# The first loads of a fused attention and feed-forward kernel: how many may be under way at once

## The chip, the cores and the metric

The kernel runs on one core of one Trainium2 chip. The metric is the device time of one execution in microseconds (us). The core has a matrix engine (PE, with its weight loads shown apart as PEld), three engines for elementwise work (DVE, ACT, POOL), a control engine SyncE (SP) that issues transfers here, and 16 DMA engines that carry them out. A load is "issued" when SP has handed it over, and "lands" when its semaphore says that all its data is in on-chip memory.

## The reference

The computation is sliding-window attention followed by a two-layer feed-forward network:

```python
# q, k, v: (8, 8, 576, 64); window 32
scores = scale * np.matmul(q, k.transpose(0, 1, 3, 2))
mask = np.abs(pos[:, None] - pos[None, :]) <= window
scores = np.where(mask, scores, -1000000000.0)
attn = softmax(scores)                    # max, exp, sum written out in full
x = np.matmul(attn, v)                    # -> (4608, 512): tokens x (head, dim)
h = x @ w_in                              # (512, 2048)
r = np.maximum(h, 0.0)
out = (s * (r * r) + b) @ w_out           # (2048, 512)
```

All inputs and the output are f32; the kernel casts what it multiplies to bf16.

## The kernel before, in words

The 4608 tokens are the eight sequences, one after the other. Attention is done per sequence in units of 128 keys; the feed-forward part runs over thirteen blocks of tokens (96, 128, 128, 160, 256, 256 and then seven of 512). The first four blocks are the first sequence, so the feed-forward part of sequence 0 can begin as soon as its attention is there, and the attention of later sequences is laid between the matrix products of earlier blocks.

The order of the work is made by a small planner. Every piece of work is a `_Task` with a stream (pe, act, dve, pool, sp), a cost in ns, a key, and the tasks it depends on (`_Graph.add`, L89). `plan` (L120) simulates the streams and puts each one's tasks in an order; `emit` (L228) turns the dependences into semaphore waits. Each stream runs its tasks strictly in the order planned, so a waiting task holds up all behind it on its engine. A transfer has in `dma` a kind, the number of packets per DMA engine and the ns per packet; their product is the planner's price of it. A transfer's wait is a wait of the engine that issues it, in most cases SP.

Tasks with a key under -100 are special: they are chained (L93, L97 to L99, L116), so they keep the order in which the program adds them. These are the first loads, all issued by SP in `attention` (L931):

- eight pairs of heads of sequence 0, q and k in turn (`load_pair`, L619, issued at L623; 288 KB, price 8 packets x 113 ns). Each goes into one of eight staging buffers `stg`, is cast to bf16 (L632, L633), turned on PE (L639) and copied out (L645, L646); `pair_scores` (L853) follows.
- two units of v (`load_v`, L561, issued at L571; 256 KB, 64 packets x 20 ns), cast at L580.
- the rest of v of sequence 0 in two halves of the partitions (`load_rows`, L584, issued at L589; 320 KB each, together 32 packets x 56 ns). DVE and POOL cast them (L592), then PE puts them in place (`place_v`, L609).
- eight loads of `w_in` (`load_weights`, L532, issued at L543; 512 KB, 16 packets x 86 ns), cast by POOL at L546.
- two tiny loads of s and b (L961).
- eight loads of `w_out` (L543, 16 packets x 85 ns), cast by POOL at L546. PE uses them first in `early` (L1066, L1074) and then in the sum over all rows at L1083.
- eight pairs of sequence 1 (L623, 8 packets x 93 ns) and five units of its v (L571, 64 packets x 17 ns, the last one 32).

The eight staging buffers serve all of the pairs and weights in turn. A load therefore waits until the cast that last read its buffer is done. Besides that, what limits how far ahead SP issues is the number of semaphores of its kind (12 for these loads) and what the DMA queue takes. What comes behind the first loads on SP are the loads of later sequences (L670, L571), transposing transfers (L685, L835) and the stores of the output (L1063).

PE's matrix products of the feed-forward part are at L1025 (`w_in`) and at L1043 (`w_out`); ACT applies the relu (L1032), DVE squares (L1034).

Of the kernel before, what the change touches and what calls it, by code (L numbers as in the profile page):

```python
# [56 lines left out]
AHEAD = {"pe": 48, "act": 180, "dve": 240, "pool": 240}  # L57


class _Task:  # L60
# [3 lines left out]
    def __init__(self, n, stream, fns, cost, lat, key, dma, slack, after):  # L64
        self.slack, self.after, self.next = slack, after, []
        self.n, self.stream, self.fns, self.cost, self.lat, self.key, self.dma = \
            n, stream, fns, cost, lat, key, dma
        self.deps, self.users = set(), []
        self.ready = self.start = self.fin = 0.0
        self.sem = self.seq = self.val = None  # L70
        self.used = False
        self.snap = self.half = self.mark = None


class _Graph:
# [3 lines left out]
    STREAMS = ("pe", "act", "dve", "pool", "sp")  # L79
    LAT = {"pe": 260.0, "act": 130.0, "dve": 110.0, "pool": 150.0, "sp": 60.0}  # L80
    MARGIN = 250.0
    RING, PUSH, CALM, ISSUE, WRITE = 112.0, 95.0, 40.0, 1400.0, 600.0

    def __init__(self, queues):
        self.queues = queues
        self.tasks, self.chain = [], None
        self.writer, self.readers = {}, {}

    def add(self, stream, fns, cost, reads=(), writes=(), key=0.0, accum=False, dma=None, waits=(),  # L89
            lat=None, slack=0.0):  # L90
        if not isinstance(fns, list):
            fns = [fns]
        after = [self.chain] if key < -100 and self.chain else []  # L93
        t = _Task(len(self.tasks), stream, fns, cost, self.LAT[stream] if lat is None else lat, key,
                  dma, slack, after)
        t.deps.update(waits)
        for a in after:  # L97
            assert a.stream == stream
            a.next.append(t)  # L99
        for r in reads:  # L100
            assert r in self.writer, r
            t.deps.add(self.writer[r])
        for w in writes:
            if w in self.writer:
                t.deps.add(self.writer[w])
            if not accum:
                t.deps.update(self.readers.get(w, ()))
        t.deps.discard(t)
        for r in reads:
            self.readers.setdefault(r, []).append(t)  # L110
        for w in writes:
            self.writer[w] = t
            if not accum:
                self.readers[w] = []
        self.tasks.append(t)
        if key < -100:  # L116
            self.chain = t
        return t

    def plan(self):  # L120
# [48 lines left out]
        def release(t):  # L169
            for u in t.users:  # L170
# [7 lines left out]
                else:  # L178
                    r = t.fin + t.lat + (self.MARGIN if u.stream == "pe" else 0.0)
                u.ready = max(u.ready, r)  # L180
# [139 lines left out]
def bass_sliding_window_symmetric__then__act_starrelu_kernel(  # L320
# [23 lines left out]
    with ExitStack() as es:  # L344
# [120 lines left out]
        def zero(stream, tile, res, cost, key=-90.0):  # L465
            add(stream, lambda e: e.memset(tile, 0.0), cost, writes=[res], key=key)

        add("dve", lambda e: e.memset(ONESW[:], 1.0), 150, writes=["ONESW"], key=-99)
        add("dve", lambda e: e.memset(RECS[:], 1.0), 250, writes=[("REC", i) for i in range(NU)], key=-58)

        add("dve", lambda e: e.memset(SROW[:], 0.0), 100, writes=[("SROW", 0), ("SROW", 1)], key=-58)
# [901 lines left out]
```

## Time and profile before

| | |
|---|---|
| median of 3 runs | 319.38 us (317.86 to 321.13) |
| the profiled execution's own time | 317.84 us |
| its span, first to last instruction | 316.1 us |
| PE busy | 300.3 us (95%) |
| DVE, ACT, POOL busy | 193.7, 141.8, 90.1 us |
| moved by DMA | 56.13 MB, mean 178 GB/s |
| `w_in` loads, issue to landing, median | 9.8 us |
| `w_out` loads, issue to landing, median | 9.6 us |
| q and k pairs, issue to landing, median | 5.3 and 4.9 us |

The profile is of one execution. Its page divides the span into 40 equal slices and gives each engine's busy share in tenths; PEclk is the granted clock of PE in tenths of full speed; DMA is the mean busy share of the 16 DMA engines. The chain of waits goes back from the last instruction, at each step to what released it; cut to a stretch, each line is start, length and what it was. "SPq" is SP's sequencer issuing a transfer, and its length contains the time for which it could not hand the transfer over. "DMA vst<-in_v_dram" is the time from an issue to a landing. In the table of engines by stretch the columns are busy time of PE, PEld, DVE, ACT and POOL, each with its number of instructions, then granted clock, DMA share and GB/s.

### The profile page before, as it was taken

The numbers are of one execution on the slowest core, as the hardware profiler recorded it, in microseconds if no ns is written. First come the engines' busy times: TensorE is split into PE (matmuls) and PEld (weight loads), VectorE is DVE, ScalarE is ACT, GpSimd is POOL, SyncE is SP. The second block draws the span as 40 slices with busy tenths as digits, with TensorE's granted clock in tenths as the row PEclk, the third lists the DMA queues.
The fourth block names the chain that finished last, engine by engine and source line by source line (L and its number), as shares of the span: only waits on it lengthen the run. The fifth ranks groups of instructions, "written<-read, shape, count | busy, mean of one in ns | idle before, by whom it ended". The sixth has DMA issues, their size and how long they took to land.

```text
span 316.1 us, 8467 instructions
## 1 busy us (share of the span) xinstructions
PE 300.3 (95%) x3588; PEld 164.6 (52%) x3632; DVE 193.7 (61%) x381; ACT 141.8 (45%) x221; POOL 90.1 (29%) x108
## 2 busy tenths in 40 slices
PE   8779999989999999999999999999999999999995
PEld 3558775466764454554444444444444444444444
DVE  4447587578884886988569485875545543333312
ACT  3836435355744674764166354444444333333300
POOL 3368955528225123241412421423000000000000
PEclk9959999999999999999999999999999999999999
DMA  7999999997996998799899999989221110001022
GB/s 229 254 382 388 386 288 276 154 191 227 261 194 169 291 178 155 232 240 158 210 292 119 183 222 301 123 151 222 73 62 53 50 46 35 33 34 36 34 94 76
DMA packets 96921, 56.13 MB, mean 178 GB/s; under 512 B 71472, under 2 KB 86064, under 8 KB 96880
## 3 DMA queue, kind: packets, MB, share of 16 engines
q1 hardware_dynamic: 96880, 55.56, 75.8%
q8 instruction: 29, 0.48, 0.7%
q14 instruction: 12, 0.10, 0.1%
HBM read 36.70 MB, written 9.44 MB: 146 GB/s over the span
## 4 chain that ended last, share of the span: by engine, by line
PE 87%; DVE 3%; SPq 3%; issue 2%; DMA 2%; ACT 2%; POOL 0%; ACTq 0%; POOLq 0%
PE w L1025 37%; PE o L1043 35%; PE avn L787 4%; PE avn L1074 2%; DMA vst<-in_v_dram 2%; PE sc L729 2%; DVE gt L1034 2%; PE o L1074 2%; ACT r L1032 1%; SPq L623 1%; SPq L589 1%; PE avn L818 1%; PE w L639 1%; PE w L609 1%; SPq L571 1%
## 5 line engine op out<-in xcount | busy, mean ns | idle before, releaser
L1025 PE MATMUL w<-xt,win 128*128 128x512 bf16 (+4 forms) x814 | 139.9, 312 | 3.1 <-issue 1.4
L1032 ACT ACTIVATE r<-w 128x512 bf16<-128x512 f32 (+2 forms) x148 | 86.3, 585 | 104.2 <-PE w L1025 83.1
L1043 PE MATMUL o<-wout,gt 128*128 128x512 bf16 (+1 forms) x510 | 123.0, 372 | 1.9 <-issue 1.4
L1034 DVE TENSOR_TENSOR gt<-r 128x512 bf16<-128x512 bf16 (+2 forms) x148 | 77.7, 530 | 74.3 <-ACT r L1032 74.2
L1025 PEld LDWEIGHTS w<-xt,win 128*128 128x128 bf16 x832 | 68.9, 98 | 52.8 <-issue 0.3
L1043 PEld LDWEIGHTS o<-wout,gt 128*128 128x128 bf16 x528 | 50.7, 98 | 55.0
L695 POOL COPY kt<-ktr 128x512 bf16<-128x512 bf16 (+1 forms) x30 | 32.3, 1078 | 41.7 <-DMA ktr<-nat 40.2
L678 POOL CAST nat<-stg 128x1024 bf16<-128x1024 f32 (+1 forms) x21 | 24.5, 1165 | 59.7 <-DMA stg<-in_q_dram 39.1
L757 ACT ACTIVATE ex<-sc 128x1024 bf16<-128x1024 f32 (+1 forms) x29 | 29.6, 1022 | 24.1 <-PE avn L787 22.1
L1059 DVE SCALAR_TENSOR_TENSOR outs<-o,sb,cvec 128x512 f32<-128x512 f32 (+1 forms) x35 | 25.4, 729 | 13.1 <-PE o L1043 13.0
L761 DVE TENSOR_TENSOR ex<-ex,mask 128x1024 bf16<-128x1024 bf16 (+1 forms) x29 | 21.6, 746 | 1.3 <-ACT ex L757 0.2
L811 DVE TENSOR_TENSOR xn<-avn,rec 128x512 bf16<-128x512 f32 (+1 forms) x31 | 21.4, 690 | 1.0
L787 PE MATMUL avn<-vb,ex 64*64 64x65 bf16 x952 | 20.9, 199 | 0.3
L787 PEld LDWEIGHTS avn<-vb,ex 64*64 64x64 bf16 x952 | 13.6, 108 | 13.3 <-issue 7.6
L580 DVE CAST vb<-vst 128x512 bf16<-128x512 f32 (+1 forms) x29 | 13.2, 459 | 2.9 <-DMA vst<-in_v_dram 2.9
L678 DVE CAST nat<-stg 128x1024 bf16<-128x1024 f32 (+1 forms) x15 | 13.6, 903 | 2.2 <-DMA stg<-in_k_dram 1.3
L729 PE MATMUL sc<-qt,kt 64*64 64x128 bf16 x440 | 11.7, 216 | 0.0
L809 DVE RECIPROCAL rec<-avn 128x8 f32<-128x8 f32 (+1 forms) x31 | 6.2, 201 | 7.0 <-PE avn L787 6.8
L826 ACT COPY xt<-avn 128x512 bf16<-128x512 bf16 (+2 forms) x14 | 7.2, 523 | 6.2 <-PE avn L818 6.2
L646 DVE COPY kt<-w 128x576 bf16<-128x576 bf16 x8 | 6.0, 755 | 5.1 <-PE w L639 5.1
L639 PEld LDWEIGHTS w<-ident,nat 64*64 64x64 bf16 x288 | 6.9, 121 | 4.3 <-issue 1.7
L546 POOL CAST win<-stg 128x1024 bf16<-128x1024 f32 x8 | 8.3, 1040 | 2.7 <-DMA stg<-in_moe_w_in_dram 2.6
(100 smaller groups left out, 153.5 us busy)
## 6 DMA issues: line engine op xcount, KB each, us to landing
out_dram<-outs SPq DMA_DIRECT2D x35, 256.0 KB, 2.5
vst<-in_v_dram SPq DMA_DIRECT2D x30, 256.0 KB, 5.3
stg<-in_q_dram SPq DMA_DIRECT2D x6, 1024.0 KB, 6.0
stg<-in_k_dram SPq DMA_DIRECT2D x6, 1024.0 KB, 10.3
stg<-in_moe_w_in_dram SPq DMA_DIRECT2D x8, 512.0 KB, 9.8
stg<-in_moe_w_out_dram SPq DMA_DIRECT2D x8, 512.0 KB, 9.6
stg<-in_q_dram SPq DMA_DIRECT2D x8, 288.0 KB, 5.3
stg<-in_k_dram SPq DMA_DIRECT2D x8, 288.0 KB, 4.9
```

Of the source, the lines that this page charges most:

```text
L678: add(eng, lambda e, x=x: e.tensor_copy(nat[0:top, 1024 * x:1024 * x + 1024].rearrange("p (i h d) -> p h i d", h=H, i=2), stg[0:top, :].re ...
L695: add("pool", lambda e, c=c, w=w: e.tensor_copy(KT[slot][:, :, c:c + w].rearrange("p a (s i) -> p a s i", i=4), KTR[slot][:, :, :, c // 4: ...
L729: fns = [lambda e, pr=pr, x=x, b=b, j=j, hp=hp: e.matmul(SC[64 * x:64 * x + 64, hp, pr * 128:pr * 128 + 128], lhsT=KT[b % 2][64 * hp:64 * ...
L757: add("act", lambda e, dst=flat_dst, src=flat_src: e.activation(dst, src, AF.Exp, bias=0.0, scale=0.125), 190 + 0.833 * 512 * len(hs), rea ...
L761: add("dve", lambda e, flat=flat, mask=mask: e.tensor_tensor(flat, flat, mask, ALU.mult), 130 + 0.53 * 512 * len(hs), reads=[("E", ei, hp, ...
L787: return [lambda e: e.matmul(av[64 * x:64 * x + 64, h, 0:D + 1], lhsT=buf[64 * g:64 * g + 64, h % 2, h // 2, c:c + 64], rhs=VB[64 * g:64 * ...
L811: add("dve", lambda e: e.tensor_tensor(XN[xi][0:p1, :].rearrange("p (a c) -> p a c", a=H), av[0:p1, :, 0:D], REC[ri][0:p1, :].rearrange("p ...
L1025: add("pe", [lambda e, g=g, kc=kc: e.matmul(wt[:, g, :], lhsT=WIN_BF[:, kc, (f0 + g) * 128:(f0 + g + 1) * 128], rhs=XT[:, kc, t0 % XR:t0 % ...
L1032: add("act", lambda e: e.activation(rt, wt, AF.Relu, bias=0.0, scale=1.0), 190 + 0.833 * ng * nt, reads=[("W", wb)], writes=[("R1", rb)], ...
L1034: add("dve", lambda e: e.tensor_tensor(GT[gs][:, f0:f0 + ng, g0:g0 + nt], rt, rt, ALU.mult), 130 + 0.53 * ng * nt, reads=[("R1", rb)], wri ...
L1043: add("pe", [lambda e, fc=fc: e.matmul(O[:, ob, 0:cn], lhsT=GT[gs][:, fc, g0:g0 + 128], rhs=WOUT_BF[:, fc, c0:c0 + cn], start=(fc == 0), s ...
L1059: add("dve", lambda e: e.scalar_tensor_tensor(OUTS[us][:, 0:cn], bank, SB128[:, 0:1], CVEC[:, c0:c0 + cn], ALU.mult, ALU.add), 200 + 1.07 ...
```

## The change

Each transfer of the chain of first loads gets one more dependence, on an earlier load of that chain. `add` goes back through the earlier loads of the chain and adds up their prices (packets x ns per packet). At the first one with which the sum passes `AHEAD` = 4500 ns it stops, and the new load waits for that one to land. Three weight loads are worth 4128 ns. Loads of 64 packets or more get no such wait, but they count in the sum of those behind them. Since SP issues the loads, it is SP that waits, before it issues.

```diff
+    AHEAD = 4500.0
...
-        self.tasks, self.chain = [], None
+        self.tasks, self.chain, self.line = [], None, []
...
         t.deps.update(waits)
+        if key < -100 and dma is not None:
+            full = 0.0
+            for other in reversed(self.line):
+                full += other.dma[1] * other.dma[2]
+                if full > self.AHEAD and dma[1] < 64:
+                    t.deps.add(other)
+                    break
+            self.line.append(t)
```

The planner sees the new dependences too, so the orders of the streams could move with them.

## The prediction, made before the changed kernel ran

> **What bounds the kernel now.** I read the page's 40 slices first, then the chain of waits cut to the first 75 us, SyncE's timeline, the DMA view of three stretches, each first load's issue and landing, and what POOL waited for.
>
> ```profile
> PE   8779999989999999999999999999999999999995
> PEclk9959999999999999999999999999999999999999
> DMA  7999999997996998799899999989221110001022
> ```
>
> The span is 316.1 us, a slice 7.9 us. After the third slice PE never leaves 8 or 9, so only the start is open to anything that loads do: the first slices are weaker on PE, and the third runs at half the granted clock. DMA is full there too.
>
> ```profile
> 7.07 3.05 SPq L589
> 10.12 0.04 issue
> 10.16 6.46 DMA vst<-in_v_dram
> 16.63 0.02 issue
> 16.65 0.02 POOLq L296
> 16.67 0.08 issue
> 16.75 0.98 POOL gt L592
> 17.73 0.05 issue
> 17.78 1.25 PE w L609 x10
> ```
>
> This is the chain (start, length, what). The one transfer on it is the second half of `load_rows`: issued at 10.16, landed at 16.63, cast by POOL, then PE. The 3.05 us of SPq before it look like a cost of issuing. They are not: SyncE sits in that instruction while the DMA engines are full, as the next rows show. The first fence is the DMA view of 0 to 20 us in half-microsecond slices, the second that of 17 to 39 us.
>
> ```profile
> DMA  0001899997799999999999999999999999999999
> GB/s 0 0 0 32 230 355 392 304 286 180 207 286 300 355 378 401 410 383 344 289 258 250 182 239 223 197 230 246 207 166 196 221 369 389 385 389 406 369 381 381
> ```
>
> ```profile
> DMA  9999999999999999999999999999999999999999
> GB/s 391 384 398 369 384 391 387 387 391 380 395 384 387 387 410 361 380 387 391 387 391 380 387 387 387 391 399 376 387 380 402 380 395 372 410 364 384 392 390 405
> ```
>
> From 2 us on the engines are full but for a dip at 4.5 to 5.5 us; the weight stream runs at 387 GB/s without a hole. The first bytes move between 1.5 and 2.0 us, and the first load's issue ended at 1.20: at most 0.8 us from issue to data.
>
> ```profile
> POOL win L546 <- DMA stg<-in_moe_w_in_dram: 2.6, 5, 1.4
> POOL gt L592 <- DMA vst<-in_v_dram: 1.9, 1, 1.9
> ```
>
> ```profile
> 12.00:16.00 4.00, 2.73 (x112) 1.72 (x110) 1.31 (x3) 3.30 (x5) 0.87 (x3) 1.00 1.08 211
> 16.00:20.00 4.00, 2.22 (x20) 1.33 (x20) 2.10 (x5) 0.67 (x2) 3.02 (x3) 0.58 1.05 384
> 20.00:24.00 4.00, 3.85 (x93) 3.13 (x92) 1.61 (x4) 1.59 (x3) 2.11 (x3) 0.56 1.05 388
> 24.00:28.00 4.00, 3.79 (x88) 3.36 (x85) 3.03 (x7) 2.64 (x5) 3.37 (x4) 1.00 1.05 387
> ```
>
> Between 17 and 45 us POOL waits for loads only for `w_in`, 2.6 us in five pieces, and 1.9 us for the rows. The second table (busy PE, PEld, DVE, ACT, POOL; then granted clock, DMA share, GB/s) places PE's weak stretch: 2.73 and 2.22 of 4 us while the rows are awaited, and the clock at about a half from 16.7 to 23.5 us.
>
> **The change, part by part.** The orders of the two builds agree line by line on PE, DVE, ACT and POOL, waits included. On SyncE the order is the same too and 25 loads gain a wait for an earlier load's landing. By the code's own prices (start pairs 8x113 = 904, v 64x20 = 1280, rows 32x56 = 1792, `w_in` 16x86 = 1376, `w_out` 1360, later pairs 8x93 = 744) a load waits for the nearest one before it with which the sum passes 4500. For weights that is the fourth back; so at its release three are still to come. Loads of 64 packets (v0, v1 and four of the next five) get no wait.
>
> *Start pairs.* The sixth, seventh and eighth wait for the first, second and third. Those landed (issue plus landing time) at 0.80+2.8 = 3.6, 1.26+3.1 = 4.4 and 1.73+4.7 = 6.4 us; the issues were at 3.14, 3.62 and 4.09. The last moves by 2.3 us to about 6.5, and behind it in SyncE's queue v0 moves from 4.88 to 6.95, v1 from 5.58 to about 7.65. Who waits for v0, v1: the casts, then the first L787. Cover: the fourth to seventh pairs landed at 7.2, 8.0, 8.7, 9.5, so the eighth, whose data can start by 6.9+0.8 = 7.7, is in time, and v0's by 7.6+0.8 = 8.4 are too: the queue then still holds the seventh and eighth pair (to 9.5 and some 10.3). Cost 0. If the cover were gone, v0's whole shift of 2.07 us would reach the rows' landing and, through POOL and PE, the end one to one. The bound below zero: the third pair landed 2.0 us after the second, the later ones 0.7 to 0.8 after each other; if that excess of 1.3 us came from the depth of the queue it would go. The DMA share in 4 to 8 us is 0.97, which leaves little of either; I take 0.
>
> *Rows and the first weights.* The rows wait for the sixth pair (3.14+5.6 = 8.7); their issue ran from 7.07 to 10.12, held by the full queue, so it still ends near 10.1. The first two `w_in` loads wait for the eighth pair and v0 (some 10.3 and 11.5, estimates between the neighbours' landings); they were issued at 10.82 and 12.33: not binding. The third waits for the rows, 16.6 instead of 12.84: 3.8 us later. Its data can start at 16.65+0.47+0.8 = 17.9; the second lands at 12.33+6.6 = 18.9, so it is there 1.0 us early. Cost 0.
>
> *The other weights.* Landings run from 21.4 (third `w_in`) to 29.59+9.3 = 38.9 (last `w_out`), 13 steps, 1.35 us each. At a release three loads, 4.05 us, are ahead; wait, issue and first bytes take 0.05+0.47+0.8 = 1.3. Spare 2.7 us. So the issues move by 4 to 7 us and the landings do not. SyncE's two scalar loads now stand between the wait at 24.2 and the first `w_out`: 0.90+0.53 us (their rows), so that one is issued at 25.7 instead of 18.85, its data due at 28.1: 1.6 us to spare. If the cover went: POOL, which casts the weights, has a reserve of 0.4 us (the last `w_in` lands at 28.1, its cast starts at 28.53) and PE behind it 0.5 (the first `w_out` cast ends at 31.10, PE's first weight load of L1074 is at 31.58); beyond 0.9 us a delay goes to the end.
>
> A rule speaks against this part. The Trainium skill, "DMA: Bandwidth & Descriptors", section "Rules for kernel authors", says to issue a DMA early and wait for its semaphore late, so that the fixed setup cost overlaps; "Anatomy of one DMA" puts that cost at about 2.0 us. The first load here took 2.8 us from issue to landing with some 0.75 of it moving, which agrees. Were the 2.0 bare at each of 12 held weight loads, an estimate by that page gives 24 us and 343 us in all; three loads ahead are what the rule's overlap asks for, and by the rows it stays hidden.
>
> *Later pairs and v.* Four of the eight pairs move (31.1 to 34.9, 32.7 to 36.2, 35.8 to 37.5, 38.5 to 38.9); due from 38.9 on in turn. The others and the last v were already issued after the landing they now wait for, because POOL freed their buffer late. Cost 0. SyncE is free at 45.6 as before, so L670 behind it does not move.
>
> **Sum.** 0+0+0+0 on the profiled execution's own 317.84 us (span 316.1 and 1.7 around it). That run lies 1.5 under the median of the three shown, 319.38; I forecast 319.4.
>
> **The rivals.**
>
> *Slower: v0's shift shows.* Place: between the eighth pair and v0. It decides once v0's first bytes come after 8.5 to 9.0, where the GB/s row begins to fall from 410 (the pairs give way to the small rows of v); my estimate is 8.4, so it is close, though the slowest engines, which set a landing, are about 1.3 us further back. Price up to 2.07: 321.5; and if PE's longer pause holds the half clock for half a stretch more (3.4 us at half speed, 1.7), 323.2.
>
> *Slower: the shallow queue loses the lead of the faster engines.* The third `w_in` landed 2.5 us after the second, the others 1.35: an excess of 1.1 us, beside an instruction fetch. The DMA view shows three such packets in 10 to 30 us and three in 25 to 45, say four more that today do not show in a landing. If all did: 4.4, less the reserve of 0.9, 3.5: 322.9. Against: three loads are ahead, over 1.1 us.
>
> *Faster: the early excess goes.* 1.3 us: 318.1; if PE's shorter pause also kept the clock whole, up to half of the 5.6 us that PE worked in the slow stretch (2.22+3.85 less 0.5 after 23.5), 2.8: 315.3. Against: fewer than eight loads were queued when the excess arose.
>
> *The waits do not bind*, because buffers freed by POOL and the full queue already hold the loads: 319.4 too. True of seven waits, not of the weights.
>
> **How the numbers follow.** Forecast 0.64, waits not binding 0.08, v0's shift 0.13, lost lead 0.08, early excess gone 0.07. A measurement of this kernel tells about 1% from no change: 316.2 and 322.6. Below lie about half of the last case and a little scatter of the first: 0.07; above, half of v0's shift, most of the lost lead and some scatter: 0.18; between, 0.75. Range 316.6 (318.1 less the 1.5 by which single runs lie under the median) to 323.2; the forecast's own, 317.9 to 321.1, is the scatter of the three runs.
>
> **What would show it.** Right: `w_in` and `w_out` land in steps of 1.35 us, issue to landing down from 9.6 to about 5.5 us, DMA still 9 in all slices of 17 to 39, the rows landing near 16.6, PE's L609 near 17.8. Wrong: holes in the DMA row at 8 to 9 or behind 17 us, POOL waiting more than 2.6 us for `w_in`, or the clock row changed in slices two to four.

## The result, and the profile after

| | before | changed |
|---|---|---|
| median of 21 runs each | 318.45 us (316.80 to 321.85) | 320.94 us (318.25 to 324.49) |
| ratio, 95% interval | | 1.0071 [1.0042, 1.0099] |
| the profiled execution's own time | 317.84 us | 320.93 us |
| its span | 316.1 us | 319.2 us |
| PE's granted clock over the span | 0.989 | 0.989 |
| rows landed | 16.63 us | 16.21 us |
| last `w_in`, first and last `w_out` landed | 28.14, 29.48, 38.89 us | 29.30, 30.61, 40.38 us |
| last pair of sequence 1 landed | 44.83 us | 48.00 us |

The change costs 0.7%, about 2.3 us: less than the 1% that a measurement of this kernel was said to tell, but here the interval excludes no change. Here and below a ratio is estimated from the runs within 1.5% of their kernel's fastest, so it can differ from the quotient of the medians, which are of all runs. The forecast was 319.4 and the range 316.6 to 323.2. All lines of the code behind the edit moved by 9, so L543 of before is L552 here, L546 is L555, L1074 is L1083, L1090 is L1099; in most of the experiments they moved by one more.

The page's 40 slices of the changed kernel, 8.0 us each:

```profile
PE   7688989989979999999999999999999999999996
PEclk9969999999999999999999999999999999999999
DMA  7999998996998997999999999987111210000022
GB/s 237 267 329 359 355 319 241 190 174 163 325 171 157 301 190 146 235 253 187 187 298 153 126 239 322 153 167 169 49 52 52 67 60 35 33 34 36 34 82 86
```

PE reads 8 in the fourth and sixth slice (24 to 32, 40 to 48 us) where it read 9; the 8 in the ninth stands in both rows (7.17 us busy in 64 to 72, 7.19 before), and the 7 in the twelfth is taken up below. Only one slice is below 9 in clock, as before: the clock has no part in the loss.

The DMA view of the changed kernel, 17 to 39 us in 40 slices:

```profile
DMA  9689999899999999999999989899789999999999
GB/s 350 227 201 276 331 391 350 313 294 302 350 406 413 410 421 380 380 272 395 398 391 361 324 305 425 291 250 261 246 298 335 376 350 354 361 372 398 402 355 398
DMA packets 3901, 7.54 MB, mean 343 GB/s; under 512 B 246, under 2 KB 246, under 8 KB 3897
```

This stretch was 9 throughout and 387 GB/s. Now there are holes at 17.5 us and between 30 and 33 us, and also slices in which the engines read 9 while they move 250 to 300 GB/s: they are busy, but with slower packets. Packet by packet, most 2 KB pieces of the weights take 0.084 to 0.095 us in both kernels. In 16.5 to 38 us none of 3844 took more than 0.3 us before; in the changed kernel 57 of 3566 did (called long below), the longest 1.45 us, in bursts. Many of the bursts follow a hole (17 to 19.5 us, 31.5 to 34); those at 26.3 and 29.3 us stand where the row reads 9.

Who pays is in what PE and DVE waited for between 26 and 52 us (total, times, longest). PE in the kernel before, PE in the changed kernel, DVE in the changed kernel:

```profile
PE sc L1090 <- DVE outs L1087: 0.3, 1, 0.3
PE avn L1074 <- DVE gt L1034: 0.3, 1, 0.3
```

```profile
PE sc L1099 <- DVE outs L1096: 1.3, 1, 1.3
PE o L1083 <- POOL wout L555: 1.2, 1, 1.2
PE w L1034 <- ACT r L1041: 0.5, 2, 0.3
```

```profile
DVE nat L642 <- DMA stg<-in_k_dram: 1.6, 2, 0.8
```

PE's first product with `w_out` waits 1.2 us for POOL's cast of the first `w_out` load. That cast ended at 32.27 us (31.10 before), because the load landed at 30.61. Some 15 us later PE waits 1.3 us, 1.0 more than before, for DVE's copies of the output. DVE does its work in the planned order, and had itself stood still 1.6 us for the pairs of sequence 1, which land up to 3.2 us later. The pairs are not the only reason for that second wait, as `win_only` shows below. The two waits add 2.2 us.

The chain of waits of the changed kernel (start, length, what), cut to 8 to 50 us:

```profile
...
9.98 6.24 DMA vst<-in_v_dram
16.21 0.02 issue
16.23 4.76 DMA stg<-in_moe_w_in_dram
20.99 0.02 issue
21.00 6.97 DMA stg<-in_moe_w_in_dram
27.98 0.02 issue
27.99 5.52 DMA stg<-in_moe_w_out_dram
33.51 0.02 issue
33.52 5.20 DMA stg<-in_moe_w_out_dram
38.73 0.02 issue
38.74 6.06 DMA stg<-in_k_dram
44.80 0.02 issue
44.82 0.64 DVE nat L642
...
```

Before, this chain held one transfer and then went over to POOL and PE. Now each load is released by the landing of another: a loop through SyncE that is gone round five times after the rows, most turns four loads long.

The profiled spans differ by 3.1 us, and not all of it is in those two waits. Matched in order, ACT's instructions at 60 to 80 us start 1.1 us later than before, and 3.3 us later from 95 us on. The second step is at DVE's casts of the next q and k (L678, here L687):

```profile
DVE nat L687 <- DMA stg<-in_k_dram: 2.1, 1, 2.1
DVE nat L687 <- DMA stg<-in_q_dram: 1.5, 1, 1.5
```

The profile of before has no such wait between 78 and 95 us. One must not put it down to the change too soon, as the experiments show.

### The profile page after: what moved, and what is told of

Read it like the earlier page. It is cut to its first block, busy times and chain, and to the rows that moved or that the text cites. A ratio compares the mean times of both kernels' runs of the same rounds, so it can differ in the third digit from the quotient of the medians.

```text
span 319.2 us, 8485 instructions
## 1 busy us (share of the span) xinstructions
PE 298.8 (94%) x3588; PEld 163.0 (51%) x3632; DVE 190.3 (60%) x381; ACT 141.6 (44%) x221; POOL 90.7 (28%) x108
## 4 chain that ended last, share of the span: by engine, by line
PE 76%; DMA 17%; DVE 2%; issue 2%; SPq 1%; ACT 1%
PE o L1052 33%; PE w L1034 32%; DMA stg<-in_k_dram 7%; DMA stg<-in_moe_w_in_dram 4%; PE avn L796 3%; DMA stg<-in_moe_w_out_dram 3%; DMA vst<-in_v_dram 2%; PE sc L738 2%; PE avn L1083 2%; PE o L1083 1%; DMA stg<-in_q_dram 1%; DVE gt L1043 1%; PE w L648 1%; PE avn L827 1%; SPq L598 0%
## 5 line engine op out<-in xcount | busy, mean ns | idle before, releaser
L687 POOL CAST nat<-stg 128x1024 bf16<-128x1024 f32 (+1 forms) x21 | 25.4, 1211 | 63.7 <-DMA stg<-in_q_dram 41.8
L704 POOL COPY kt<-ktr 128x512 bf16<-128x512 bf16 (+1 forms) x30 | 31.5, 1050 | 40.3 <-DMA ktr<-nat 38.9
L766 ACT ACTIVATE ex<-sc 128x1024 bf16<-128x1024 f32 (+1 forms) x29 | 29.7, 1023 | 23.9 <-PE avn L796 21.9
L687 DVE CAST nat<-stg 128x1024 bf16<-128x1024 f32 (+1 forms) x15 | 11.0, 736 | 4.5 <-DMA stg<-in_k_dram 3.0
L555 POOL CAST win<-stg 128x1024 bf16<-128x1024 f32 x8 | 8.3, 1042 | 4.2 <-DMA stg<-in_moe_w_in_dram 4.1
L1083 PE MATMUL o<-wout,gt 128*128 128x512 bf16 x25 | 7.4, 379 | 1.8 <-POOL wout L555 1.2
L1083 PE MATMUL avn<-wout,gt 128*128 128x512 bf16 x31 | 8.7, 380 | 0.2 <-issue 0.2
```

Of the source, the lines that this page charges most:

```text
L687: add(eng, lambda e, x=x: e.tensor_copy(nat[0:top, 1024 * x:1024 * x + 1024].rearrange("p (i h d) -> p h i d", h=H, i=2), stg[0:top, :].re ...
L704: add("pool", lambda e, c=c, w=w: e.tensor_copy(KT[slot][:, :, c:c + w].rearrange("p a (s i) -> p a s i", i=4), KTR[slot][:, :, :, c // 4: ...
L766: add("act", lambda e, dst=flat_dst, src=flat_src: e.activation(dst, src, AF.Exp, bias=0.0, scale=0.125), 190 + 0.833 * 512 * len(hs), rea ...
L1083: add("pe", [lambda e, fc=fc, bank=bank, gs=gs, g0=g0: e.matmul(bank, lhsT=GT[gs][:, fc, g0:g0 + 128], rhs=WOUT_BF[:, fc, :], start=(fc == ...
```

## Experiments

Three theories stood at first. *Lost lead*: a load lands when the slowest of the 16 DMA engines is through; the faster ones run ahead and finish all that has been issued, so that three loads ahead of the slowest are too few for them. *Start*: the held start pairs and rows delay v0. *Waits*: SyncE's 25 waits or its longer path cost in themselves. The first four kernels stood beside one set of runs of the kernel before (median 318.55 us, 35 runs).

**start_only**: only loads priced 113 or 56 ns per packet, the first pairs and the rows, get the new wait.

```diff
+    HELD = (113.0, 56.0)
-                if full > self.AHEAD and dma[1] < 64:
+                if full > self.AHEAD and dma[1] < 64 and dma[2] in self.HELD:
```

> Only the first pairs of heads and the rows of v keep their new waits; weights, scalars, later pairs and later v have none. Lost-lead theory (the loss comes from the weight stream: with three loads ahead the faster DMA engines run dry, lose their lead, and an instruction fetch of about 1.1 us on one of them then shows in a landing): ratio to the kernel before 0.998 to 1.001, rows landing near 16.2 to 16.7 us, the last pair of sequence 1 landing near 44.8 as before. Start theory (the loss is the later issue of the first two units of v): ratio 1.005 or more, rows landing over 17 us.

Measured: 318.81 us, ratio 0.9996 [0.9968, 1.0024]. The rows landed at 15.95 us, the last pair of sequence 1 at 45.22, and no weight packet was long. The start theory falls.

**weights_only**: as above, but for the weights alone.

```diff
+    HELD = (86.0, 85.0)
```

> Only the sixteen weight loads keep their new waits. Lost-lead theory: the greater part of the loss is here, ratio 1.004 to 1.009, with one to three landing steps of 2.2 to 2.8 us instead of 1.35 between the third w_in and the last w_out, the last pair of sequence 1 landing 1.5 to 3.5 us later than 44.8. Start theory: ratio 0.999 to 1.001. Late-pairs theory (the waits of the pairs of sequence 1 make the loss): ratio under 1.003.

Measured: 320.17 us, ratio 1.0051 [1.0018, 1.0085]. Last pair at 46.74; of the sixteen weight landings four came 1.8 to 2.2 us after the one before, the others about 1.35; 48 long packets. Most of the loss is here.

**later_only**: the pairs and v of sequence 1, and the two tiny loads of s and b, which come ahead of `w_out`; the weights themselves get no wait.

```diff
+    HELD = (15.0, 93.0, 17.0)
```

> Only the two scalar loads, the pairs of sequence 1 and the last v of sequence 1 keep their new waits. Lost-lead theory: ratio 1.000 to 1.003, since only four of these loads are really held and the queue ahead of them is deep until then. Late-pairs theory: ratio 1.004 or more, the step to the first pair 2.2 us instead of 0.7 as in the changed kernel.

Measured: 320.17 us, ratio 1.0017 [0.9980, 1.0053]. What SyncE waited for between 15 and 30 us:

```profile
SPq L971 <- DMA stg<-in_moe_w_in_dram: 6.1, 1, 6.1
SPq L553 <- POOL mask L485: 1.1, 1, 1.1
```

L971 is a tiny load. It waits for the fifth `w_in` load, and behind it on SyncE stands all of `w_out`: the first one is issued at 24.66 us (18.85 before). The DMA view of 23 to 33 us, a quarter of a microsecond per slice:

```profile
DMA  9999999995778999975969799999789899999798
GB/s 393 385 393 393 393 377 393 360 377 197 180 188 205 311 360 344 434 287 180 197 123 213 205 336 328 385 336 352 270 344 418 328 369 360 369 361 295 188 385 295
```

The engines run partly dry at 25.3 us and again at 27.5 (an instruction fetch of 1.1 us falls into the first hole), the second `w_out` lands 3.87 us after the first, the last pair at 47.92, as late as in the changed kernel. The first `w_out` landed at 28.54, before the long step, and PE did not wait for its cast. What this kernel loses is not settled: the interval reaches from no loss to 0.5%, and the median of 320.17 us is that of `weights_only`. So whether it matters which load is late is not shown by it.

**ahead_8500**: the whole change with `AHEAD` = 8500, six weight loads ahead.

```diff
-    AHEAD = 4500.0
+    AHEAD = 8500.0
```

> All waits, with the bound at 8500 ns instead of 4500: six weight loads ahead instead of three. Lost-lead theory: the faster engines keep their lead, ratio 0.999 to 1.002, weight landings in steps of 1.35 us with at most one longer step, as before. A theory by which the waits themselves cost on SyncE (22 of the 25 remain): ratio near 1.006 as with 4500.

Measured: 318.94 us, ratio 0.9983 [0.9953, 1.0013]. The built program still has 19 of the 25 new waits (the expectation says 22), and nine loads are issued within 0.02 us of the landing that they wait for. The weights land in steps of 1.35 us, the last pair at 44.63. The waits cost nothing that shows where enough is ahead; the theory of the waits falls.

The next four (before: 317.93 us, 23 runs) varied the depth, and tried the two halves of what was left of the theory: that the lead is lost, and that the lateness is then paid.

**weights_4100**: weights alone, `AHEAD` = 4100. Two loads are then ahead at the release of a `w_in` and of the first three `w_out`. For the last five `w_out` it is still three, since three loads at 1360 ns make 4080.

```diff
-    AHEAD = 4500.0
+    AHEAD = 4100.0
+    HELD = (86.0, 85.0)
```

> Only the weight loads are held, with the bound at 4100 ns: two loads still to come at a release (2.7 us) instead of three. Lost-lead theory: the less is ahead, the more is lost; ratio 1.008 to 1.025 against 1.005 with three, weight steps mostly over 1.35 us, DMA under 330 GB/s between 17 and 39 us. A theory by which each wait costs a fixed amount, whatever is ahead: 1.005 again.

Measured: 323.68 us, ratio 1.0146 [1.0100, 1.0192], three times the loss of `weights_only`. The DMA view of 17 to 39 us:

```profile
DMA  6798779967899999989689899999998999999997
GB/s 227 209 257 235 242 276 324 313 160 227 294 290 354 402 421 384 372 294 253 175 197 268 313 302 339 328 328 361 369 339 324 406 402 384 335 346 391 324 298 305
DMA packets 3523, 6.80 MB, mean 309 GB/s; under 512 B 226, under 2 KB 226, under 8 KB 3519
```

Holes nearly throughout; most landings are 1.7 to 2.3 us apart and the last pair comes at 50.53.

**ahead_6000**: the whole change with four loads ahead.

```diff
-    AHEAD = 4500.0
+    AHEAD = 6000.0
```

> All waits with the bound at 6000 ns: four weight loads ahead at a release. Lost-lead theory: between three (1.007) and six (0.998), ratio 1.000 to 1.004, at most two long steps in the weight stream. Fixed-cost theory: 1.005 or more.

Measured: 317.90 us, ratio 1.0000 [0.9973, 1.0028]. The same view:

```profile
DMA  9999999999999999999799999999999999999999
GB/s 387 417 365 384 380 391 387 387 387 387 380 395 410 365 369 391 384 309 324 268 380 402 380 398 421 376 391 395 384 406 372 384 384 402 376 385 389 391 392 399
DMA packets 4314, 8.40 MB, mean 382 GB/s; under 512 B 292, under 2 KB 292, under 8 KB 4308
```

One hole at 27.5 us is left, one step of 1.65 us, 5 long packets. With one load more the loss is gone: for this stream the edge lies between three and four.

**extra_loads**: the kernel before, with two more loads of 512 KB behind the last `w_in`, issued by SyncE like the others but with semaphores of their own, into a part of a buffer that is not used yet. It makes the stream late without holding anything back.

```diff
+            for x in (0, 1):
+                spare = GT[1][:, 8 + 4 * x:12 + 4 * x, :] ...
+                add("sp", lambda e, spare=spare, src=src: e.dma_start(spare, src), 10.0, ...
+                    key=nxt(), dma=("x", 1, 2.0))
```

> The kernel before, no new waits, with two more 512 KB loads (a part of w_in once more, into a buffer that is not yet used) behind the last w_in: 2.7 us more of DMA time and nothing else. It prices lateness by itself. If lateness of the stream is carried on because the DMA engines stay full until about 87 us: pairs of sequence 1 land 2.7 us later, ratio 1.005 to 1.010. If the reserves named in the prediction (0.9 us) take most of it: 1.003 to 1.006. If weights and pairs had room to spare: 0.999 to 1.002.

Measured: 320.82 us, ratio 1.0084 [1.0053, 1.0114]: 2.7 us for 2.7 us more of DMA, with full engines and no long packet. The first `w_out` landed 4.08 us after the last `w_in`. Two of PE's waits between 26 and 52 us are those of the changed kernel, the first and the third line:

```profile
PE o L1080 <- POOL wout L546: 1.2, 1, 1.2
PE w L1031 <- issue: 0.7, 1, 0.7
PE sc L1096 <- DVE outs L1093: 0.7, 1, 0.7
```

So lateness alone, from the first `w_out` on, brings a loss of this size.

**fetch_moved**: the changed kernel with PE's warm-up cut to one wide product and 40 narrow ones, to move the instruction fetches (16 KB packets of 0.9 to 1.3 us) against the landings.

```diff
-                                      start=True, stop=True)] * WARM,
+                                      start=True, stop=True)] * 1 +
+            [lambda e: e.matmul(W[:, 1, 0:1], lhsT=ONESW[:, :], rhs=ONESW[:, 0:1], start=True, stop=True)] * 40,
```

> The changed kernel with PE's five warming products replaced by one and forty of one column, so that PE's instruction fetches fall about 2 us earlier. If an instruction fetch on a DMA engine without lead makes the long steps, they move with it: the long step of the seventh w_in (2.7 us, fetch at 24.7) comes one or two loads earlier. If the long steps belong to certain loads or waits, they stay at the third and seventh w_in and the first pair.

Measured in one run: 321.77 us. The fetch that was to move stayed at 24.8 us (24.7), so this is inconclusive as a test of moving. The fifth `w_in` landed 2.52 us after the fourth, at 25.69, and a fetch from 24.8 to 25.7 overlaps the end of that step. Whether a step can be long without a fetch is shown better by `weights_only`: its fifth `w_in` landed 2.19 us after the fourth, at 24.26, and no fetch ran between 18.5 and 24.4 us. The stretches of `fetch_moved` (length, busy PE, PEld, DVE, ACT, POOL, clock, DMA share, GB/s):

```profile
16.00:18.00 2.00, 0.48 (x32) 0.26 (x24) 0.58 (x2) 0.69 (x1) 0.48 (x1) 0.77 0.56 191
18.00:20.00 2.00, 1.45 (x14) 1.06 (x16) 1.53 (x4) 0.16 (x1) 1.75 (x3) 0.50 0.68 179
...
22.00:24.00 2.00, 1.91 (x58) 1.49 (x54) 0.18 (x1) 1.03 (x2) 1.78 (x2) 0.53 0.94 258
```

The rows came late here (17.40), the third `w_in` was held on them, and for 4 us the share was 0.56 and 0.68. In this kernel, as in `weights_only`, long steps come with engines that are partly empty; a fetch is not needed.

The last four (before: 318.10 us, 35 runs) split the weights, and tried whether an earlier stream gains.

**win_only** and **wout_only**: the wait for `w_in` alone, and for `w_out` alone.

```diff
+    HELD = (86.0,)
```

> Only the eight w_in loads are held, three loads ahead. Run-dry theory (engines that have finished all that was issued wait, and their next packets are slow): about half of what holding all sixteen weights costs, ratio 1.001 to 1.004, long packets and DMA under 360 GB/s between 17 and 24 us and none behind. If it is the w_out side alone: 0.999 to 1.001.

```diff
+    HELD = (85.0,)
```

> Only the eight w_out loads are held. Run-dry theory: the other half, ratio 1.001 to 1.004, DMA whole (387 GB/s) until about 25 us and with dips behind. If it is the w_in side alone: 0.999 to 1.001.

Measured: `win_only` 320.41 us, ratio 1.0038 [1.0001, 1.0074]; `wout_only` 318.90 us, 1.0021 [0.9992, 1.0051]. The stretches of `win_only`, then those of `wout_only`:

```profile
17.00:21.00 4.00, 3.99 (x54) 2.90 (x54) 1.72 (x4) 1.60 (x3) 2.08 (x2) 0.57 0.88 287
21.00:25.00 4.00, 3.73 (x128) 3.21 (x123) 2.98 (x7) 2.15 (x4) 2.41 (x3) 1.00 0.99 313
```

```profile
17.00:21.00 4.00, 4.00 (x44) 2.80 (x42) 1.55 (x4) 1.60 (x3) 2.78 (x3) 0.50 1.05 391
21.00:25.00 4.00, 3.74 (x124) 3.19 (x120) 2.13 (x6) 1.76 (x4) 3.06 (x4) 0.89 1.05 385
25.00:29.00 4.00, 3.71 (x79) 3.50 (x71) 2.53 (x7) 2.72 (x6) 3.60 (x7) 1.00 1.04 376
29.00:33.00 4.00, 3.92 (x46) 2.94 (x43) 2.97 (x4) 1.76 (x5) 3.69 (x6) 1.00 1.02 358
```

Each loses rate where its own waits are. Those of `w_in` come first, at 17 to 25 us, and make the first `w_out` late (31.34). Those of `w_out` come after it (28.28); no loss is shown, and up to 0.5% is not excluded. PE's waits between 26 and 52 us in `win_only`:

```profile
PE w L1035 <- issue: 1.8, 1, 1.8
PE sc L1100 <- DVE outs L1097: 1.0, 1, 1.0
PE o L1084 <- POOL wout L556: 0.9, 1, 0.9
```

DVE waits for no pair in this stretch here, and still PE waits 1.0 us for DVE's copies, 0.7 more than before. So most of PE's second wait comes along with the late `w_out` and is not the pairs' doing. The first line, a wait for nothing that the profile shows, is longer than either; 1.1 us of the kind stand in `rows_split` and `fewer_bytes`, which lose nothing.

**fewer_bytes** and **rows_split**, both on the kernel before: the last two `w_out` loads carry 8 of their 512 columns; and the rows go in four transfers, alternating between the halves of the partitions.

```diff
+            cut = 8 if which == "out" and i == 3 else 512
-            add("sp", lambda e: e.dma_start(stg, src), 600.0, writes=[("STG", si)], key=key,
+            add("sp", lambda e: e.dma_start(stg[:, :, 0:cut], src[:, :, 0:cut]), 600.0, writes=[("STG", si)], key=key,
```

> The kernel before, but the last two w_out loads carry 8 of 512 columns each, so the output is not the reference's: 2.7 us less DMA time and nothing else. If the time follows the DMA stream in both directions, as 2.7 us more gave 1.0084: ratio 0.990 to 0.995. If PE or POOL is next in line at once: 0.997 to 1.000.

```diff
-            add("sp", [lambda e, hp=hp: e.dma_start(dst[64 * hp:64 * hp + 64, :, :], src[hp]) for hp in (0, 1)],
+            add("sp", [lambda e, hp=hp, y=y: e.dma_start(dst[64 * hp:64 * hp + 64, 2 * y:2 * y + 2, :], src[hp][:, 2 * y:2 * y + 2, :])
+                       for y in (0, 1) for hp in (0, 1)],
```

> The kernel before, with the rows of v loaded in four transfers that change between the lower and the upper 64 partitions instead of two that do so once. The row packets took about 100 ns and up to 130 while 2304-byte packets took 93. If two halves of the partitions under way together go faster: the rows and the whole stream behind them land 0.5 to 1.2 us earlier, ratio 0.995 to 0.999. If not: 0.999 to 1.002.

Measured: `fewer_bytes` 318.66 us, ratio 0.9998 [0.9969, 1.0026]; `rows_split` 318.57 us, 1.0014 [0.9981, 1.0048]. In the first the last `w_out` landed at 36.54, 2.35 us earlier, but the last pair at 44.75 (44.83), because SyncE waits for POOL to free the staging buffers. It does so as long in the kernel before, whose row is the third:

```profile
SPq L624 <- POOL wout L547: 6.0, 5, 1.5
SPq L624 <- POOL mask L513: 2.4, 2, 1.4
SPq L623 <- POOL wout L546: 6.0, 5, 1.5
```

Less data at the end of `w_out` saves nothing, since the loads behind it wait for POOL. The first `w_out` was not made earlier by it (29.31). In the second the rows landed at 15.9 us, within the 15.70 to 16.63 of the kernels that load them unsplit (17.40 in `fetch_moved` aside), and no gain is shown. It also has ten weight packets of 0.34 to 0.46 us and two long steps (1.85 and 1.52 us), with nothing held and the engines at 9 throughout: long packets are not a mark of held loads alone.

**All runs in one table.** Landings in us, PE's wait for the first `w_out` cast, and what PE waited for DVE's output copies beyond the 0.3 us of before, each in the profiled run; then the timed ratio.

| kernel | first `w_out` | last `w_out` | last pair | PE on `w_out` | PE on DVE | ratio |
|---|---|---|---|---|---|---|
| wout_only | 28.28 | 38.15 | 45.01 | 0 | 0 | 1.0021 |
| later_only | 28.54 | 41.29 | 47.92 | 0 | 0.4 | 1.0017 |
| rows_split | 28.50 | 38.04 | 44.11 | 0 | 0 | 1.0014 |
| ahead_6000 | 28.80 | 38.55 | 44.45 | 0.4 | 0 | 1.0000 |
| ahead_8500 | 29.29 | 38.71 | 44.63 | 0 | 0 | 0.9983 |
| fewer_bytes | 29.31 | 36.54 | 44.75 | 0 | 0 | 0.9998 |
| before | 29.48 | 38.89 | 44.83 | 0 | 0 | |
| start_only | 29.64 | 39.01 | 45.22 | 0 | 0 | 0.9996 |
| weights_only | 30.35 | 40.25 | 46.74 | 1.2 | 0.7 | 1.0051 |
| changed | 30.61 | 40.38 | 48.00 | 1.2 | 1.0 | 1.0071 |
| win_only | 31.34 | 40.96 | 46.86 | 0.9 | 0.7 | 1.0038 |
| extra_loads | 31.62 | 41.59 | 47.50 | 1.2 | 0.4 | 1.0084 |
| fetch_moved | 31.88 | 41.79 | 49.45 | 1.2 | 0.7 | one run |
| weights_4100 | 32.06 | 44.38 | 50.53 | 1.8 | 1.0 | 1.0146 |

Every timed kernel whose first `w_out` landed after 30 us is slower, with an interval above 1; none that had it by 29.7 is shown to be. PE's two waits add up to 2.2 us in the changed kernel (2.3 timed), 1.9 in `weights_only` (1.6 timed), 1.6 in `win_only` (1.2), 0.4 in `later_only` (0.5). For `extra_loads` (1.6 against 2.7) and `weights_4100` (2.8 against 4.6) they are too little; there PE waits in other places too. Since one profile stands against a median, the close ones are partly luck.

A surer reading matches each kernel's ACT instructions in order with those of before. At 46 to 60 us they start later by 0.6 us in `weights_only`, 1.5 in the changed kernel, 1.6 in `win_only` and `extra_loads` and 4.3 in `weights_4100`. In the six kernels whose interval holds 1 and whose pairs are not late it is -1.2 to 0.2 us. `later_only`, whose interval holds 1 too, is at 0.8, among those that lose. The place at 30 us is not a fixed one either: in `ahead_6000` PE waited 0.4 us for a first `w_out` that landed at 28.80, because it had come 1.2 to 1.5 us further than before.

DVE's wait at L687 around 85 us, on the other hand, is no part of this that could be shown. In the profiled runs it is 3.6 us in the changed kernel and 2.5 in `extra_loads`, but also 2.7 in `ahead_6000`, 1.8 in `ahead_8500` and 1.4 in `start_only`, which lose nothing, and it is absent in `weights_only`, which does. It varies from kernel to kernel without following the time, and the profile of before happened to have none. Whether a late stream makes it likelier stays open.

## Why the prediction was right or wrong

The time lies in the range and within 1%, but the likeliest case, no cost, was wrong: the changed kernel is slower by a small amount that the interval sets apart from none. Some of the nearness is luck. The forecast of no cost stood on the median of three runs, 319.38; the median of 21 is 318.45, so the number came 0.9 us nearer to 320.94 than the reasoning did.

**Start pairs: right.** Cost 0 taken; `start_only` measured 0.9996 [0.9968, 1.0024]. The rows landed 0.4 us earlier in the changed kernel, no later; neither v0's shift nor the early excess showed in the time.

**Rows and the first weights: right for the landing, wrong in the reason.** The third `w_in` was issued at 16.23 instead of 12.84 and landed at 20.99, 0.4 us earlier than before. But its data was not there "1.0 us early" for all engines: they fell to 201 GB/s at 18 us, and the long packets began around there.

**The other weights: this step failed**, where it said that at a release three loads, 4.05 us, are ahead, that wait, issue and first bytes take 1.3, "Spare 2.7 us. So the issues move by 4 to 7 us and the landings do not." The issues moved by 3.3 to 6.6 us, and from the seventh `w_in` on the landings moved too, by 1.0 to 1.5 us. Issue to landing came down to 5.5 us for `w_out`, as expected, and to 6.6 for `w_in`; most steps stayed at 1.3 to 1.4. With three ahead the fifth and seventh `w_in`, the third and last `w_out` took 1.57, 2.72, 1.62 and 1.65 us instead of about 1.35 (the third `w_in` took 2.3, as it had before). From the third `w_in` to the last `w_out` a step is 1.49 us on average instead of 1.345; 13 steps of 0.147 make 1.9 us. With six ahead it is 1.348, with four 1.367, with two and then three 1.825.

What was mis-sized is the spare of 2.7 us. It counts from a landing, and some of the three loads ahead has already been moved by then. The trace counts packets, not engines: in the kernel before, from the third `w_in` to the sixth `w_out`, the packets that had moved beyond the loads already landed were worth 1.8 to 2.0 us of the stream at each landing. Taken from 4.05, and less 1.3 for wait, issue and first bytes, this leaves about 0.8 us of spare for the mean engine, an estimate, and less for one that is ahead of the mean. Such an engine can then have nothing left to do. That single engines ran out is argued and not seen. In the changed kernel this mean lead is 0.5, 0.9, 1.1 and 1.6 us at the landings ahead of the third, fifth and seventh `w_in` and the third `w_out`, the long steps, but 0.9 to 1.4 ahead of several steps of 1.3 too, so it does not say which step will be long.

The step's reserve was nearer the mark. It said that the first `w_out`'s cast can come 0.5 us later before PE stands still: a landing at about 30.0 us. The table's edge lies between 29.64 and 30.35. The further 0.4 us that it gave POOL did not show: that load landed 1.13 us later, and its cast ended 1.17 us later.

**Later pairs and v: wrong for the landings.** Four of the eight pairs were to move, at cost 0, with landings due in turn behind the last `w_out`. That load came 1.5 us later than before, and the last pair 3.2 us, so only about half is inherited. The rest arose at the pairs themselves: the first one, held until 36.09 us and issued at 36.11, landed 2.21 us after the last `w_out` instead of 0.72. In `weights_only`, where the pairs are not held, the last pair comes 6.49 us behind the last `w_out`, in the changed kernel 7.62 (5.94 before). What this costs is not settled: PE's second wait is 0.3 us longer than in `weights_only`, and the ratios of the two, 1.0071 and 1.0051, overlap.

**The rivals.** *The shallow queue loses the lead of the faster engines* is nearest to what happened. It had 0.08 and a price of 3.5 us; measured are 2.3. Of its two parts the shallow queue is shown by the dose: two (then three) and three loads ahead give 1.0146 and 1.0051 with the weights alone, four and six give 1.0000 and 0.9983 with all waits. The other part, that each loss is an instruction fetch coming to light, can hold only for some: the seventh `w_in`, which took 2.72 us, stands beside a fetch at 24.7, but in `weights_only` a step of 2.19 us has none. The argument against this rival, that three loads are ahead and a fetch takes 1.1 us, was the same count as in the failed step. *The waits do not bind* was wrong for the weights, as the text said.

**The rule that spoke against this part** had the sign right, where the forecast had no cost. The Trainium skill, "DMA: Bandwidth & Descriptors", section "Rules for kernel authors", asks to issue early and wait late; these runs agree in sign, 1.0071 with three loads ahead and no loss shown with four. The estimate of 24 us from its fixed cost was ten times too high. (The section "Anatomy of one DMA" gives its 2.0 us for transfers that GpSimd issues, while SyncE issues these; the first load's 2.8 us less 0.75 of moving is this case's own figure.) The same page, section "Why a DMA increments its semaphore by 16 and not by 1", says that up to 16 engines finish a transfer independently and that only the full count means that all has landed. By that, a landing is the report of the slowest engine. No run here shows the engines one by one, but the lead of 1.8 to 2.0 us in the mean agrees with it.

**What would show it.** Of the signs named for "wrong", holes in the DMA row and POOL waiting more than 2.6 us for `w_in` came, the latter with 4.1 us. The second sign is a weak one: `fewer_bytes` has 3.2 us and loses nothing.

```profile
POOL win L555 <- DMA stg<-in_moe_w_in_dram: 4.1, 7, 1.3
POOL gt L601 <- DMA vst<-in_v_dram: 1.5, 1, 1.5
```

**What stays open.** Why weight packets take 0.3 us and more in bursts, instead of about 0.09, was not settled; most bursts come with an empty stretch, those of `rows_split` do not. How far each single engine is ahead could not be read from the trace. Whether a late first `w_out` or the late stream behind it is what costs is not settled, since `later_only` does not separate them. No kernel tried is shown to beat the one before.

## What to carry to other kernels

If loads are held back by the landing of earlier ones, do not take the work issued beyond a landing as all still to come: part of it has already moved, here 1.8 to 2.0 us of 4.05 in the mean. Here a full stream wanted four loads of 512 KB ahead, and three lost 11% of its rate. Then look for the first consumer with little reserve, here 0.5 us at the first `w_out`: the kernels that were late there lost, and for holes behind that load no loss was shown. Before a second wait in a profile is added to the bill, see whether kernels of unchanged time show it too.

## What the runs showed of the hardware that was not expected

- Slow weight packets come in bursts: 0.3 to 0.75 us in the changed kernel, the longest 1.45, mostly around stretches in which engines are empty, against 0.084 to 0.095 in a full stream. In `later_only` the share fell to between 0.5 and 0.9 twice, for about 1 and 1.5 us, and the step there was 2.5 us longer than usual.
- The DMA share tells little of this. 17 to 39 us have a share of 0.99 at 343 GB/s in the changed kernel and 1.05 at 387 before: slow packets count as busy. GB/s is the column to read.
- One load of a few bytes, held on SyncE for 6.1 us, delayed every large load behind it.
- With full engines 2.7 us more of transfers ahead of `w_out` cost 2.7 us [1.7, 3.6], while 2.7 us less at its end changed the time by nothing that shows [-1.0, 0.8].
